# Attention and a feed-forward layer on one core: the order of the first 1040 operations from an explicit table

## The chip, the cores and the metric

The kernel runs on one core of a Trainium2 chip. A core has a matrix engine (TensorE, PE in the profile), a vector engine (VectorE, DVE), a scalar engine (ScalarE, ACT), a general engine (GpSimd, POOL) and an engine for synchronisation (SyncE, SP). Each works through its own list of instructions in the order in which the program gave them; they wait for each other through semaphores. Transfers are issued from the queues of POOL, SP and ACT and run on 16 DMA engines. PE multiplies from on-chip memory (SBUF) into its accumulators (PSUM), which DVE and ACT read.

The metric is the device time of one run in microseconds, as the median of several runs. A profile is one further execution with the hardware profiler on; its times are those of that execution.

## The reference

```python
def _attn_ref(q, k, v):                       # (8, 12, 448, 64) each
    S = q.shape[2]
    scale = 1.0 / np.sqrt(q.shape[-1])
    scores = scale * np.matmul(q, k.transpose(0, 1, 3, 2))
    attn = np.maximum(scores, 0.0) ** 2 / S
    return np.matmul(attn, v).astype(np.float32)

def _moe_ref(x, w_in, w_out):                 # (3584, 768), (768, 2048), (2048, 768)
    h = x @ w_in
    inv_sqrt2 = np.float32(1.0 / np.sqrt(2.0))
    g = 0.5 * h * (1.0 + erf(h * inv_sqrt2))
    return (g @ w_out).astype(np.float32)
```

`reference` runs the attention, moves the heads beside each other to a matrix of 3584 tokens by 768, and puts it through the two products with the exact GELU between them. Attention has a squared ReLU in place of a softmax.

## The kernel before

**Attention.** Eight batches are taken one after the other, each as three groups (`g`) of four heads. For a group, seven QK steps (`fn_qk`, line 674) each write four blocks of scores, 64 keys by 448 queries, into a PSUM buffer `ps`: four matmuls of 64x64 x 448 that run side by side, one in each quarter of the array. A ReLU with scaling follows, on ACT (`fn_relu`, line 686) or on DVE (line 688), into a buffer `a_sq`; DVE squares it in place (line 695). An AV step (line 735) sums 28 matmuls in the same 64x64 division into a PSUM buffer `pav`, and two copies (lines 451 on DVE and 453 on ACT) take it to `xT`. The buffers `ps` and `pav` come from one ring of three, named "w". Batch 0 is taken in half rows. The operands `qT` and `kT` of batches 0 and 1 are transposed on PE (lines 545 and 573); those of later batches by DMA transposes on the SP queue (line 600), after loads on the POOL queue (lines 407, 486 and 504). A small copy on POOL (`gate`, line 641) holds back the next loads until a group's transposes have landed.

**Feed-forward.** The first product of batches 0 to 4 is plain: six matmuls of 128x128 x 448 into a PSUM buffer `psh` (line 787), then GELU on ACT (line 797). The last three batches use a scheme with seven products in place of eight (Strassen's, after Winograd): products into `pb` (line 931), sums on DVE (line 965), GELU (line 974). The second product goes the same way in groups of 256 tokens (`add_group`): products p1, p6, p2, p7, p5, p4, p3 into `pso` (line 1101), sums v2, v3, c22, c21, c12 on DVE (line 1135) and copies. Its operands need sums of hidden rows (`s_sb`, line 1082) and of weights (`t_sb`, line 1038). The first 256 tokens are done plainly (line 1196). Results collect in a ring of three buffers `osb` and go out by stores on the SP queue (line 1062). `pso`, `psh` and the transposes share a ring of two PSUM buffers, "f".

**Division of the array.** Every operation of PE has a mode: "A" for QK and AV (64x64), "T" for transposes (128x64), "F" for the feed-forward (128x128). A list for PE (`pe_q`) weaves the feed-forward of earlier batches between the QK and AV steps of a later one.

**The order.** All work is first collected as 1427 `Op` objects (plus 8 fills, short matmuls on zeros that occupy PE early on) with their possible engines, durations, dependences and buffers. `Scheduler.run` then places them. `place` first takes the words of `ORDER`: P, A, D, G or S for PE, ACT, DVE, POOL or SP with the operation's number, or Z with the size of a fill. What the table doesn't name is placed by `pick` and `pick_pe`, which take the operation that can start first by the planner's own clock, with `SWITCH` added on PE at a change of mode. `run` does this `PASSES` times, each time with due times from the last placing (`deadlines`), keeps the best, sorts it by time, and only then calls each operation's function, which writes the instructions. So the planner's costs matter for the order alone. In the kernel before the table has 264 words, for the first part of the kernel.

Of the kernel before, what the change touches and what calls it, by code (L numbers as in the profile page):

```python
# [47 lines left out]
RELU_DVE = 0.8  # L48
DMA_FREE = 3.05
DMA_LAT = 2.13  # L50
SWITCH = 0.09
LEAD = 8
HALF_M = 6
PASS_BIAS = -0.4
SUM_BIAS = -0.3
# [1 line left out]
LEADS = {}  # L57
SHARES = (1.3, 1.0, 1.0, 1.0, 1.0, 1.0)
LAST = 256
PASSES = 5  # L60
PULL = 0.15
PULL_IN = 0.45
NEAR = 0.25
# [17 lines left out]


ORDER = """
A10 P11 D13 A16 D12 P17 D18 P14 G0 P42 A15 G1 P39 A40 G2 P19 D43 G3 D44 P21 A22 P33 D20 P36 G4
Z128 P54 G5 P25 A37 P23 A55 G6 P51 D34 P48 A24 A49 D26 D35 D56 D41 D38 A52 Z1056 P69 D70 G7
Z1024 P57 Z992 P63 A58 D53 Z448 P45 D50 P66 G8 G9 D59 A64 A46 P27 P31 D28 G117 D32 A67 D65 D68
A47 G118 P60 P78 G119 A61 P29 D30 G120 P81 A79 A82 D62 G121 G122 Z1088 P93 A94 D71 P108 Z544
P84 A85 Z992 P75 D109 A76 D83 D80 P72 P90 D73 P129 D95 P105 A74 G123 P102 A91 D130 A106 P131
D86 D77 G124 D132 P141 D92 A103 P111 P96 G125 A112 P165 P143 A97 D104 P156 D107 A166 A157 P87
D113 D98 P99 D110 D88 G126 A142 D89 P114 P174 P133 D100 G127 A101 A175 D115 D116 P159 A144  # L90
P168 D134 G128 P171 D169 A160 P135 D172 D173 D170 A136 G147 P251 P192 D193 P186 P162 A252 P145
D176 A163 A146 P243 P253 P180 P195 A187 A244 P198 P137 A254 G148 D164 D158 P139 G149 G150 A181
D167 G151 A199 D161 P183 D196 A184 P177 D138 D140 D188 G152 P189 P219 P245 P247 D194 A178 A190
S231 A220 D185 A179 P207 P216 A246 S229 D182 P213 D191 D197 P261 A248 A208 S232 P263 S228 D200
A214 P222 D217 P204 D221 D209 P201 D215 A262 A223 A264 P210 A211 P265 G153 S230 A266 P259 A260
P249 P255 D218 D205 A202 A250 A203 P257 D224 G154 A256 D206 D212 P225 P267 G155 A258
"""


# [14 lines left out]
class Scheduler:  # L114
# [99 lines left out]
    def run(self, fixed):  # L214


        best = None
        for _ in range(PASSES):
            self.reset()
            self.place(fixed)  # L220
            self.deadlines()
            end = self.free["PE"]
            if best is None or end < best[0]:
                best = (end, list(self.log))
        self.open, self.log = [], best[1]


        def at(x):
            est, op, eng = x
            if eng not in ("ACT", "DVE"):  # L230
                return est
            return est + next(lat for e, _, lat in op.engines if e == eng)

        for est, op, eng in sorted(self.log, key=at):
            op.fn(eng)

    def deadlines(self):
# [97 lines left out]
def kernel(  # L335
# [119 lines left out]
    def e_copy(n, psum=4):  # L455
# [4 lines left out]
    sch = Scheduler({"w": 3, "a": NA, "f": 2, "osb": 3, "s1": 1, "s2": 1, "s3": 1, "s4": 1,  # L460
                     "p": 1})
# [384 lines left out]
    def add_wsums(after, done):  # L846

        last = [o[0] for (bb, *_), o in list(Tq.items()) + list(Tk.items()) if bb == B - 1]
        last += [o for (bb, *_), o in QK.items() if bb == B - 2]
        add, sub = mybir.AluOpType.add, mybir.AluOpType.subtract  # L850

        def one(n, m0, op, a, b, deps):
            m1 = m0 + M1 // 2
            return sch.add(
                (("DVE", 0.95, 1.07),),
                lambda e: V.tensor_tensor(wcols(n, m0, m1), a(m0, m1), b(m0, m1), op=op),
                deps + last + after,
            )

        def part(i, j):  # L860
            return lambda m0, m1: wpart(i, j, m0, m1)

        def summed(n):
            return lambda m0, m1: wcols(n, m0, m1)

        for m0 in (0, M1 // 2):
            s1 = one(1, m0, add, part(0, 1), part(1, 1), [])
            s2 = one(2, m0, sub, summed(1), part(0, 0), [s1])
            s4 = one(4, m0, sub, part(1, 0), summed(2), [s2])
            s3 = one(3, m0, sub, part(0, 0), part(0, 1), [s1] + done)  # L870
            WS[m0] = {1: s1, 2: s2, 3: s3, 4: s4}
# [48 lines left out]
    def add_block(b, m4, y, ms, bank, x, t, TS, xs, old, half):  # L920

        tmp = {}

        def product(name, left, right, deps, first=False):
            def fn(e):
                if first and name not in bank:
                    bank[name] = w_pp.tile([128, 2, NB], F32, tag="w", name="pb")
                for z, m in enumerate(ms):
                    w, mm = left(m)
                    for k in range(K1):  # L930
                        nc.tensor.matmul(  # L931
                            bank[name][:, y, z * HS : z * HS + HS],
                            w[:, k, bass.ts(mm, 128)],
                            right()[:, k],
                            start=first and k == 0 and z == 0,
                            stop=k == K1 - 1,
                            skip_group_check=not first or z > 0,
                        )

            d = 2 * K1 * (HS / 2400 + 0.0025)  # L940
            return sch.add(
                (("PE", d, d + 0.24),), fn, deps, mode="F",
                need=("w",) if first and y == 0 else (),
            )

        def plain(i, j):
            return lambda m: (wpart(i, j), m)

        def summed(n):
            return lambda m: wtile(n, m)  # L950

        def ps(name):
            return bank[name][:, y, :S]

        def get(name):
            if name not in tmp:
                tmp[name] = apool.tile([128, S], F32, tag="a", name="part")
            return tmp[name]

        def passed(name, to, other, deps, need=()):  # L960
            def fn(e):
                if other is None:
# [40 lines left out]
        c12.frees = ("w",)  # L1003
        g12 = gelu(lambda: get("t"), 0, 1, [c12], ("a",))
        for name, o in (("a", c11), ("b", c21), ("c", c12)):
            bank.setdefault(("end", name), []).append(o)
        return [p1, p6, p2, p7, p5, p4, p3]
# [25 lines left out]
    def add_tsums():  # L1033

        def sub(n, c, a, b, deps):
            return sch.add(
                (("DVE", 0.95, 1.07),),
                lambda e: V.tensor_sub(tsum(n)[:, c], a()[:, c], b()[:, c]), deps, bias=TSUM_BIAS,
            )

# [24 lines left out]
    def add_group(g):  # L1065
# [13 lines left out]
        def sum_op(n, op, a, b, deps):  # L1079
            def fn(e):  # L1080
# [1 line left out]
                V.tensor_tensor(box["s", n], a(), b(), op=op)  # L1082

            o = sch.add(
                (("DVE", 0.69, 0.8),), fn, deps, need=(f"s{n}",), bias=SUM_BIAS
            )
            mine.append(o)
            return o
# [200 lines left out]
    o = early("ACT", lambda: nq[0][:, :4, : HC * D], q32, 5.3)  # L1289
# [70 lines left out]
    for b in range(2, B):  # L1360
# [9 lines left out]
        if b + 1 < B:  # L1370

            n = {2: 2}.get(b, 1)
# [91 lines left out]
```

## Time and profile before

| | us |
|---|---|
| median of 3 runs | 371.42 |
| lowest, highest | 371.38, 372.08 |
| the profiled execution | 371.65 |
| span of its profile | 369.5 |

Durations of single instructions that the prediction uses, by shape:

| line, engine | what | count | mean ns |
|---|---|---|---|
| L686 ACT | ReLU, 128x896 from PSUM | 138 | 924 |
| L688 DVE | ReLU, 128x896 from PSUM | 29 | 1089 |
| L695 DVE | square, 128x896 | 167 | 619 |
| L451 DVE | cast `pav` to `xT`, 128x448 | 38 | 617 |
| L453 ACT | the same | 4 | 535 |
| L453 ACT | copy `pso` to `osb` or `p_sb`, 128x384 | 17 | 478 |
| L1135 DVE | sum of `pso` and `p_sb` into `osb` | 39 | 556 |
| L1082 DVE | sum of hidden rows `s_sb` | 52 | 683 |

The page of a profile gives the busy time of each engine and its share of the span, then the chain of work that ended last, followed back from the last instruction. Lines of a timeline give start, length, engine, line, operation, and in brackets the idle time before it with what ended it. A DMA-issuing instruction on the SP queue is shown as SPq. Matmuls are pipelined, and their ends in the profile are modelled: a matmul's start is observed, its end is not.

### The profile page before, as it was taken

How to read it: one execution, taken by the hardware profiler on the slowest of the kernel's cores; microseconds unless marked ns; L12 is line 12 of the kernel's file. 1: busy time of each engine (PE TensorE's matmuls, PEld its weight loads, DVE VectorE, ACT ScalarE, POOL GpSimd, SP SyncE). 2: the span in 40 equal slices, each digit the busy share in tenths (PEclk: the TensorE clock that was granted, in tenths of full speed). 3: DMA queues.
4: the chain of work that ended last, by engine and by line, in shares of the span. 5: the costliest groups of instructions: out<-in, count | busy, mean ns of one | idle time of the engine just before them, and what ended most of it. 6: DMA issues, size and time to landing. Idle time of an engine off the chain costs nothing.

```text
span 369.5 us, 8514 instructions
## 1 busy us (share of the span) xinstructions
PE 361.4 (98%) x3573; PEld 222.9 (60%) x3573; DVE 280.9 (76%) x479; ACT 204.8 (55%) x313; POOL 63.5 (17%) x103
## 2 busy tenths in 40 slices
PE   8999999999999999999999999999999999999994
PEld 7675645455544455554455544447876897688663
DVE  3999930789887688997688979998778558765862
ACT  4998954755377745777764578853540353045200
POOL 8666304230112114040212000000000000000000
PEclk9999999999999999999999999999999999999998
DMA  9999999999999999999999992002002301210232
GB/s 174 195 202 204 202 185 167 194 202 171 159 217 208 163 163 204 189 167 162 180 169 117 164 200 64 2 1 87 2 0 87 88 0 46 87 40 2 85 87 85
DMA packets 89269, 47.27 MB, mean 128 GB/s; under 512 B 55312, under 2 KB 85776, under 8 KB 89232
## 3 DMA queue, kind: packets, MB, share of 16 engines
q0 software_dynamic: 32912, 22.47, 44.7%
q1 hardware_dynamic: 55952, 23.76, 36.6%
q8 instruction: 28, 0.46, 0.5%
q10 hardware_dynamic: 368, 0.51, 0.4%
q14 instruction: 9, 0.07, 0.1%
HBM read 45.61 MB, written 11.01 MB: 153 GB/s over the span
## 4 chain that ended last, share of the span: by engine, by line
PE 86%; DMA 3%; SPq 3%; DVE 2%; issue 1%; POOL 1%; ACT 1%; DVEq 0%; POOLq 0%; ACTq 0%
PE pso L1101 29%; PE psh L787 25%; PE pb L931 13%; PE ps L674 9%; PE pav L735 7%; SPq L600 3%; DMA nq<-in_q_dram 2%; PE pso L1196 1%; ACT a_sq L686 1%; DMA out_dram<-osb 1%; DVE osb L1135 1%; PE tp L573 1%; DVE part L965 1%; POOL v_sb L504 1%; PE tp L545 0%
## 5 line engine op out<-in xcount | busy, mean ns | idle before, releaser
L686 ACT ACTIVATE a_sq<-ps 128x896 bf16<-128x896 f32 x139 | 120.1, 921 | 32.0 <-PE ps L674 31.8
L695 DVE TENSOR_TENSOR a_sq<-a_sq 128x896 bf16<-128x896 bf16 (+1 forms) x169 | 98.2, 616 | 4.5 <-ACT a_sq L686 3.4
L787 PE MATMUL psh<-xT,win_sb 128*128 128x448 bf16 (+1 forms) x516 | 96.3, 340 | 0.0
L787 PEld LDWEIGHTS <-win_sb 128*128 128x128 bf16 x516 | 48.0, 98 | 45.1 <-issue 9.2
L797 ACT ACTIVATE h_sb<-psh 128x448 bf16<-128x448 f32 x80 | 43.8, 549 | 29.9 <-PE psh L787 29.9
L1101 PEld LDWEIGHTS <-s_sb 128*128 128x128 bf16 x424 | 40.4, 98 | 27.3 <-issue 3.2
L688 DVE TENSOR_SCALAR a_sq<-ps 128x896 bf16<-128x896 f32 (+1 forms) x30 | 32.1, 1073 | 24.8 <-PE ps L674 24.7
L965 DVE TENSOR_TENSOR part<-pb,part 128x448 f32<-128x448 f32 x60 | 34.6, 620 | 21.5 <-PE pb L931 21.5
L674 PE MATMUL ps<-qT,kT 64*64 64x448 bf16 (+1 forms) x756 | 48.6, 336 | 1.2 <-ACT a_sq L686 0.4
L1101 PEld LDWEIGHTS <-h_sb 128*128 128x128 bf16 x312 | 29.9, 98 | 21.8 <-issue 3.3
L1101 PE MATMUL pso<-wout_sb,s_sb 128*128 128x384 bf16 (+2 forms) x216 | 38.1, 320 | 0.1
L1101 PE MATMUL pso<-wout_sb,h_sb 128*128 128x384 bf16 x208 | 38.1, 326 | 0.0
L1101 PE MATMUL pso<-t_sb,s_sb 128*128 128x384 bf16 x208 | 38.1, 326 | 0.0
L735 PE MATMUL pav<-a_sq,v_sb 64*64 64x448 bf16 (+1 forms) x756 | 36.5, 329 | 0.0
L674 PEld LDWEIGHTS <-kT 64*64 64x64 bf16 x756 | 18.6, 105 | 24.7 <-issue 17.8
L974 ACT ACTIVATE h_sb<-part 128x448 bf16<-128x448 f32 x36 | 20.1, 578 | 20.2 <-DVE part L965 19.9
L451 DVE CAST xT<-pav 128x448 bf16<-128x448 f32 (+1 forms) x45 | 24.4, 581 | 7.9 <-PE pav L735 7.6
L1135 DVE TENSOR_TENSOR osb<-pso,p_sb 128x384 f32<-128x384 f32 x39 | 21.7, 556 | 9.8 <-PE pso L1101 5.3
L931 PEld LDWEIGHTS <-win_sb 128*128 128x128 bf16 x288 | 27.6, 98 | 2.3 <-issue 0.4
L735 PEld LDWEIGHTS <-v_sb 64*64 64x64 bf16 x756 | 21.0, 107 | 11.8 <-issue 1.6
L641 POOL COPY gate<-qT 128x16 bf16<-128x16 bf16 x15 | 4.3, 284 | 113.8 <-DMA qT<-nq 113.8
L931 PEld LDWEIGHTS <-ws 128*128 128x128 bf16 x216 | 20.7, 98 | 0.0
(61 smaller groups left out, 294.6 us busy)
## 6 DMA issues: line engine op xcount, KB each, us to landing
nk<-in_k_dram POOLq DMA_DIRECT2D x23, 224.0 KB, 6.7
nq<-in_q_dram POOLq DMA_DIRECT2D x21, 224.0 KB, 8.6
v_sb<-in_v_dram POOLq DMA_DIRECT2D x5, 672.0 KB, 15.0
out_dram<-osb SPq DMA_DIRECT2D x8, 336.0 KB, 3.0
v_sb<-in_v_dram POOLq DMA_DIRECT2D x9, 224.0 KB, 8.2
out_dram<-osb SPq DMA_DIRECT2D x7, 288.0 KB, 3.2
out_dram<-osb SPq DMA_DIRECT2D x8, 240.0 KB, 3.0
win_sb<-in_moe_w_in_dram POOLq DMA_DIRECT2D x8, 192.0 KB, 8.5
```

The source lines that it names most:

```text
L451: V.tensor_copy(dst, src)
L674: nc.tensor.matmul(ps[64 * j : 64 * j + 64, e, x * w : x * w + w], kT[r, g, i * 128 + 64 * j : i * 128 + 64 * j + 64], moving, start=True, ...
L686: A.activation(ar, ps, AF.Relu, scale=c_att)
L688: V.tensor_scalar(ar, ps, c_att, 0.0, op0=mybir.AluOpType.mult, op1=mybir.AluOpType.max,)
L695: V.tensor_mul(box["a2"][:, :, :used], ar, ar)
L735: nc.tensor.matmul(pav[0][o2 : o2 + 64, e, :w], vt[b][r, 2 * g + e, bass.ts(i, D)], box["a2"][r, y, o : o + w], start=(i == 0), stop=(i == ...
L787: nc.tensor.matmul(ph[:, x * n : x * n + n], win_sb[:, kd, bass.ts(m + x, 128)], xT[b][:, kd, c], start=(kd == 0), stop=(kd == KD - 1),)
L797: A.activation(h_ring()[:, m : m + nm, o + c.start : o + c.stop], box[0][:, :S].rearrange("p (x n) -> p x n", x=nm), AF.Gelu,)
L931: nc.tensor.matmul(bank[name][:, y, z * HS : z * HS + HS], w[:, k, bass.ts(mm, 128)], right()[:, k], start=first and k == 0 and z == 0, st ...
L965: V.tensor_add(get(to), ps(name), get(other))
L1101: nc.tensor.matmul(box[bank][:, n0:n1], left()[:, kf], right()[:, kf, n0:n1], start=bool(need) and kf == 0, stop=kf == K2 - 1, skip_group_ ...
L1135: V.tensor_add(out()[:, n0:n1], box[bank][:, n0:n1], other()[:, n0:n1])
```

## The change

The table `ORDER` becomes a new one of 1435 words: 1427 operations and the same 8 fills. Operations stand in it in a new sequence up to about the 1040th; from there on they stand as the planner had placed them before. Some operations change engine between ACT and DVE, as their letters say. The other edits are to the planner: `SWITCH` from 0.09 to 0.11, `PASSES` from 5 to 1, lower durations for three kinds of sums on DVE, no sort ahead of writing the instructions, and one more dependence, of the second half of a product bank on the first.

```diff
-SWITCH = 0.09
+SWITCH = 0.11
...
-PASSES = 5
+PASSES = 1
...
 ORDER = """
-A10 P11 D13 A16 D12 P17 D18 P14 G0 P42 A15 G1 P39 A40 G2 P19 D43 G3 D44 P21 A22 P33 D20 P36 G4
-Z128 P54 G5 P25 A37 P23 A55 G6 P51 D34 P48 A24 A49 D26 D35 D56 D41 D38 A52 Z1056 P69 D70 G7
...
-P249 P255 D218 D205 A202 A250 A203 P257 D224 G154 A256 D206 D212 P225 P267 G155 A258
+G0 G1 G2 G3 G4 G5 G6 A10 P11 D13 A16 P17 G7 D12 P14 D18 P42 P39 G8 P19 A15 P21 D43 P33 P36 D44
+A40 D20 Z128 A22 P54 G9 P25 P23 A37 D34 P51 D26 P48 A55 Z1056 D35 A24 P69 D56 Z1024 D41 A49
...
+S403 D428 P431 G409 D344 D338 S389 D341 P440 P437 D332 P345 S404 D430 A438 P443 D441 P446 S405
...
+G879 A830 G880 D827 S875 P733 G881 A907 D828 D831 P912 D825 P921 P832 D745 A913 P909 A732 D922
+P924 P735 D734 A833 A925 P737 A910 D743 A834 P936 D914 P918 P933 D736 P739 D738 S741 D744 A934
...
+P1419 D1418 S1424 P1420 D1421 S1425 D1422 S1426
 """
...
-        def at(x):
-            est, op, eng = x
-            if eng not in ("ACT", "DVE"):
-                return est
-            return est + next(lat for e, _, lat in op.engines if e == eng)
-
-        for est, op, eng in sorted(self.log, key=at):
+        for _, op, eng in self.log:
             op.fn(eng)
...
-                (("DVE", 0.95, 1.07),),
+                (("DVE", 0.86, 1.07),),
...
-            return sch.add(
-                (("PE", d, d + 0.24),), fn, deps, mode="F",
+            o = sch.add(
+                (("PE", d, d + 0.24),), fn, deps + bank.get(("first", name), []), mode="F",
                 need=("w",) if first and y == 0 else (),
             )
+            if first:
+                bank["first", name] = [o]
+            return o
```

More of the change, by code (lines that the diff above doesn't have):

```diff
@@ L83 @@
 ORDER = """
-A10 P11 D13 A16 D12 P17 D18 P14 G0 P42 A15 G1 P39 A40 G2 P19 D43 G3 D44 P21 A22 P33 D20 P36 G4
-Z128 P54 G5 P25 A37 P23 A55 G6 P51 D34 P48 A24 A49 D26 D35 D56 D41 D38 A52 Z1056 P69 D70 G7
[L86 to L95, printed above, removed]
@@ L96 @@
-P249 P255 D218 D205 A202 A250 A203 P257 D224 G154 A256 D206 D212 P225 P267 G155 A258
+G0 G1 G2 G3 G4 G5 G6 A10 P11 D13 A16 P17 G7 D12 P14 D18 P42 P39 G8 P19 A15 P21 D43 P33 P36 D44
+A40 D20 Z128 A22 P54 G9 P25 P23 A37 D34 P51 D26 P48 A55 Z1056 D35 A24 P69 D56 Z1024 D41 A49
+P57 Z992 D38 A52 P63 Z448 G117 D70 P45 A58 D53 P66 A64 D50 P27 A46 G118 P31 D59 P60 D28 A67
+G119 D32 A47 P78 P29 D65 G120 A61 P81 Z1088 D68 D30 A79 P93 D62 P108 Z544 D71 A82 P84 Z992
+G121 A94 P75 D109 P72 G122 D83 A85 P90 P129 D80 G123 D73 A76 P105 A74 P102 D95 G124 P131 D130
@@ new lines @@
+A91 P141 D86 A106 D77 P111 P96 D132 A103 P165 P143 D92 A112 D104 D107 A97 P156 D113 P87 G125
+D98 A166 P99 D110 G126 D88 A157 P114 A142 D100 A89 P174 G127 A101 P168 D115 P133 A144 P135
+A116 G128 D175 P171 P159 A169 D134 P251 D136 D170 A160 P145 D158 A172 D167 A252 P162 P186 D176
+P192 P243 A146 D161 G147 D173 A187 G148 P253 D193 A163 A244 D164 P195 G149 P180 P198 P137 A254
+G150 P139 D196 A181 P183 P177 G151 D138 A199 D140 A184 P189 P219 P245 D178 G152 A190 D185 P247
+G153 D194 A220 D179 A246 G154 P213 D188 P222 P204 P263 D221 A248 G155 D197 A214 D200 P265 D191
@@ new lines @@
+A205 D182 A264 P261 A223 A266 P216 D224 S231 P207 P201 D206 A262 A208 S229 P210 P259 D209 A217
+D215 S232 P255 D211 A260 P249 D212 D218 A256 D202 P225 A203 S228 A250 P257 S230 A226 P267 D227
+A258 P348 S234 A268 P350 S233 A349 P352 G237 A351 G238 P354 S235 A353 G239 P288 S236 P294 P282
+P358 A355 G240 G241 D289 P356 D283 A359 P360 D295 A357 D290 P306 P279 P276 D296 P362 A361 D307
+P364 D280 A363 P366 D277 A365 P368 A367 P370 A369 P300 P285 P291 G242 P372 A371 G269 D286 A292
+P374 G270 D284 A373 G271 P318 P303 D301 P312 G272 P376 D308 A375 G273 A304 D319 P378 D278 A377
@@ new lines @@
+P380 D313 A379 D293 G274 D314 D390 P382 D305 G275 D302 A381 D391 D287 D281 P330 P309 P297 S398
+D392 A331 D320 P315 S399 P384 D393 A298 D396 A310 S401 A383 D417 P387 D394 D419 A385 D311 A299
+D395 A316 D317 P324 P321 D418 A325 P333 D397 P327 A388 P421 D420 D322 S400 A328 D323 P423 D326
+A334 D422 S386 P339 P336 P342 P425 D424 D329 A343 D335 P427 S402 A426 D337 P429 G407 A340 G408
+S403 D428 P431 G409 D344 D338 S389 D341 P440 P437 D332 P345 S404 D430 A438 P443 D441 P446 S405
+P433 D432 A346 D347 A444 P509 A447 D434 P511 D439 G410 D448 S406 A510 G411 P449 D442 P452 G412
@@ new lines @@
+P455 P513 D562 A512 S435 D445 S436 A453 P515 D454 A450 A514 P517 D456 D451 P464 D457 P461 P458
+S541 A465 P467 D462 A518 P470 G413 S542 P519 A516 G414 A459 G415 P521 D471 S543 G416 D472 A520
+P523 D466 A468 D460 S544 A522 P479 D560 P476 P473 D469 P525 A524 D463 A477 P527 D480 A474 D478
+A526 P529 D475 D481 A528 P488 P485 P482 S545 A489 P494 D486 A530 P491 P531 D487 D483 P533 D495
+A532 S546 P535 D496 A484 D561 A492 P503 D490 P500 A534 P497 D493 P537 A536 G550 G551 S547 P564
+D498 G552 A538 D504 S548 P539 D499 A501 G553 A565 D505 P600 G554 D502 P603 P506 G555 S549 A601
@@ new lines @@
+P606 D604 A540 P609 P566 D563 A507 D602 P568 D607 D567 P570 D610 A569 A508 P572 D571 P624 P612
+P618 S704 P574 D580 D608 A613 D573 P576 S705 G556 A619 D581 G557 D582 P627 S706 D575 P615 G558
+P584 D614 G559 D577 S578 A616 D611 P586 S707 D605 A628 D617 A625 P636 D620 P630 S579 A585 P621
+D629 G713 A631 D637 P633 G714 P588 D587 S708 G715 A622 D626 D623 A634 P639 P642 P648 D583 P590
+D638 A640 D635 A589 D632 P592 D641 A643 D591 P651 A649 S709 D644 P657 P645 D593 A652 P666 D658
+P654 P594 D653 A646 D659 A655 D650 P596 A647 D667 S710 D595 P660 P766 P663 P672 D597 A661 D767
@@ new lines @@
+P674 A664 S711 D662 A673 D656 P676 D668 A675 D665 P772 P769 P669 S712 G716 D773 A770 P763 S598
+P775 A677 G717 P678 S599 D670 G718 A764 D771 P680 G719 D723 A776 S867 D768 A679 P790 P778 D765
+A671 P781 G720 P682 A681 D777 G721 D791 P684 G722 S868 D725 A683 P686 D779 A782 A685 P688 D783
+D780 D774 P787 P793 P784 D724 S869 A788 P799 D794 A687 P796 P690 A689 D795 D789 A797 P692 D798
+A691 P694 A693 P696 A785 A695 S870 P698 A786 A800 P802 P811 A697 P805 D801 P700 A699 A803 D812
+P702 S871 D792 A806 D804 P814 P817 D807 P808 A815 S872 P823 D818 A701 P820 P727 G876 D816 A703
@@ new lines @@
+G877 D809 S873 A821 G878 D726 P729 A810 D819 A728 D822 P826 D813 A824 P829 S874 P906 P731 D730
+G879 A830 G880 D827 S875 P733 G881 A907 D828 D831 P912 D825 P921 P832 D745 A913 P909 A732 D922
+P924 P735 D734 A833 A925 P737 A910 D743 A834 P936 D914 P918 P933 D736 P739 D738 S741 D744 A934
+P747 D908 G882 A937 D740 G883 P749 D938 A919 S978 G884 D935 A748 G885 D926 P942 P930 S742 P915
+P751 D750 A931 D943 S979 P753 D920 A916 A752 D746 P755 D923 S980 D911 D944 P948 P945 D917 P927
+D888 A949 D754 P939 P757 D950 A928 D886 D756 P759 A946 D887 A940 D758 A929 P835 D932 D947 D941
@@ new lines @@
+S981 P957 P954 P951 A836 D958 A955 P960 P963 D760 P837 D959 A961 D952 P839 D956 A953 S982 A838
+P966 D964 P972 P969 D962 P841 A840 S983 D889 A973 D965 P843 S984 A842 D967 P847 A970 S985 A844
+P845 D971 D968 S761 D974 P990 P987 D1067 P975 S986 A991 P993 D988 A846 P996 S762 P849 D992
+A848 D1068 A976 D1070 P851 A997 D989 A850 P853 A994 A977 D995 P1005 P1002 A852 P999 P855 A854
+D1006 A1003 P859 D1004 A1000 D998 A856 P857 D1007 D1001 P1011 P1014 P1008 D1059 A858 A1012
+P1017 D1015 P1026 P861 A1009 D1063 A860 P863 D1060 A1018 D1010 P1020 A1027 P1029 D1061 P1023
@@ new lines @@
+A862 P865 D1016 A864 D1019 P890 A1021 D1028 D1022 A866 P892 D1062 A1024 A891 D1013 P894 D1025
+A1030 D1069 D893 P1035 D1031 P1038 P1032 D1064 A895 A1036 D1066 P1041 D1037 A1039 P1044 P896
+D1033 A1042 D1034 D1040 P898 A1045 D1043 D897 P1047 D1046 P1050 P1053 P900 D899 A1048 D1139
+P902 D1049 A1051 D1140 A1054 P1071 D1052 D1055 P1056 D901 S904 A1072 D903 S905 P1088 D1141
+P1073 D1057 P1090 A1089 D1058 P1143 D1074 D1091 P1075 D1065 P1092 A1144 P1077 D1142 A1076
+D1179 P1094 A1093 D1180 P1079 D1078 P1096 D1095 P1145 D1080 D1097 A1081 P1082 D1181 A1098
@@ new lines @@
+P1099 D1146 P1085 D1083 P1102 D1100 A1084 P1105 D1086 A1101 P1122 D1103 A1087 P1107 D1182
+A1106 P1124 A1123 P1147 A1104 D1108 D1125 P1109 P1126 A1148 P1111 A1110 P1128 A1127 P1113
+D1112 P1130 D1129 P1149 D1114 D1131 A1115 P1116 A1132 P1133 D1150 P1119 D1117 P1136 D1134
+A1118 P1151 D1120 A1135 D1137 A1121 P1153 D1291 A1138 D1292 D1152 P1155 D1159 D1154 S1157
+P1163 D1160 D1156 S1158 P1165 D1161 D1164 P1167 D1162 D1166 D1293 P1169 D1294 A1168 P1171
+D1170 P1173 D1253 D1172 P1175 D1251 D1174 S1177 P1183 D1252 P1200 D1176 S1178 P1185 A1184
@@ new lines @@
+D1254 P1202 A1201 P1255 D1186 D1203 P1187 P1204 A1256 P1189 A1188 P1206 A1205 P1191 D1190
+P1208 D1207 P1257 D1192 D1209 A1193 P1194 A1210 P1211 D1258 P1197 D1195 P1214 D1212 A1196
+P1217 D1198 A1213 P1234 D1215 A1199 P1219 A1218 P1236 A1235 P1259 A1216 D1220 D1237 P1221
+P1238 A1260 P1223 A1222 P1240 A1239 P1225 D1224 P1242 D1241 P1261 D1226 D1243 A1227 P1228
+A1244 P1245 D1262 P1231 D1229 P1248 D1246 A1230 P1263 D1232 A1247 D1249 A1233 P1265 A1250
+D1264 P1267 D1271 D1266 S1269 P1275 D1272 D1268 S1270 P1277 D1273 D1276 P1279 D1274 D1278
@@ new lines @@
+P1281 D1280 P1283 D1282 P1285 D1365 D1284 P1287 D1363 D1286 S1289 P1295 D1364 P1312 D1288
+S1290 P1297 A1296 D1366 P1314 A1313 P1367 D1298 D1315 P1299 P1316 A1368 P1301 A1300 P1318
+A1317 P1303 D1302 P1320 D1319 P1369 D1304 D1321 A1305 P1306 A1322 P1323 D1370 P1309 D1307
+P1326 D1324 A1308 P1329 D1310 A1325 P1346 D1327 A1311 P1331 A1330 P1348 A1347 P1371 A1328
+D1332 D1349 P1333 P1350 A1372 P1335 A1334 P1352 A1351 P1337 D1336 P1354 D1353 P1373 D1338
+D1355 A1339 P1340 A1356 P1357 D1374 P1343 D1341 P1360 D1358 A1342 P1375 D1344 A1359 D1361
@@ L97 @@
+A1345 P1377 A1362 D1376 P1379 D1383 D1378 S1381 P1387 D1384 D1380 S1382 P1389 D1385 D1388
+P1391 D1386 D1390 P1393 D1392 P1395 D1394 P1397 D1405 D1396 P1399 D1403 D1398 S1401 P1407
+D1404 D1400 S1402 P1409 D1406 D1408 P1411 D1410 P1413 D1412 S1423 P1415 D1414 P1417 D1416
+P1419 D1418 S1424 P1420 D1421 S1425 D1422 S1426
 """
@@ L1036, in sub @@
             return sch.add(
-                (("DVE", 0.95, 1.07),),
+                (("DVE", 0.86, 1.07),),
                 lambda e: V.tensor_sub(tsum(n)[:, c], a()[:, c], b()[:, c]), deps, bias=TSUM_BIAS,
@@ L1084, in sum_op @@
             o = sch.add(
-                (("DVE", 0.69, 0.8),), fn, deps, need=(f"s{n}",), bias=SUM_BIAS
+                (("DVE", 0.6, 0.8),), fn, deps, need=(f"s{n}",), bias=SUM_BIAS
             )
```

## The prediction

> **What bounds the kernel now.** I read the page's busy times first, then the busy times by stage, then the chain of work that ended last, and at its two odd places the timeline.
>
> ```profile
> span 369.5 us, 8514 instructions
> ...
> PE 361.4 (98%) x3573; PEld 222.9 (60%) x3573; DVE 280.9 (76%) x479; ACT 204.8 (55%) x313; POOL 63.5 (17%) x103
> ...
> PE 86%; DMA 3%; SPq 3%; DVE 2%; issue 1%; POOL 1%; ACT 1%; DVEq 0%; POOLq 0%; ACTq 0%
> ```
>
> TensorE is the bound. No other engine can set the end on average, so an order gains only by making PE's own work shorter or by taking out a wait of PE. The stages differ (columns: stretch, length, then busy time of PE, weight load, DVE, ACT and POOL, clock, DMA share, GB/s):
>
> ```profile
> 0.00:32.00 32.00, 29.60 (x609) 22.08 (x613) 25.35 (x51) 25.77 (x38) 22.36 (x36) 1.00 1.23 192
> 32.00:99.00 67.00, 67.00 (x612) 36.29 (x609) 46.20 (x71) 41.83 (x65) 18.79 (x30) 1.00 1.26 188
> 99.00:250.00 151.00, 150.03 (x1420) 76.32 (x1419) 128.32 (x215) 101.95 (x143) 22.41 (x37) 1.00 1.05 146
> 250.00:369.50 119.50, 114.76 (x939) 88.22 (x936) 81.00 (x145) 35.28 (x68) 0.00 (x0) 0.99 0.18 54
> ```
>
> PE is full in all but the first stage and the tail; DMA is full up to 250 us. The chain's pieces (start, length, what) show what a change of array division costs; psh is in 128x128, ps in 64x64:
>
> ```profile
> 54.33 10.32 PE psh L787 x54
> ...
> 107.05 0.69 PE ps L674 x12
> 107.74 3.51 PE psh L787 x18
> 111.25 0.50 PE ps L674 x8
> ```
>
> From 18 to 54 psh matmuls takes 6.81 us more, 0.189 each; 18 of them should take 3.41 but take 3.51, so 0.10 belongs to the run and not to its matmuls. Four more ps matmuls take 0.19; eight should take 0.38 but take 0.50, so 0.12. A run in 128x128 and a run in 64x64 together carry 0.22 to 0.23 for two changes: **0.113 us a change**.
>
> Now the wait that matters most for where a saving counts (chain pieces again):
>
> ```profile
> 84.91 6.86 SPq L600
> ...
> 91.87 2.97 SPq L600
> ...
> 94.93 0.53 SPq L1062
> ...
> 95.52 3.17 DMA out_dram<-osb
> ...
> 98.78 0.56 DVE osb L1135
> ```
>
> and the timeline of PE after it:
>
> ```profile
> 97.64 1.46 PE L1101 MATMUL pso<-t_sb,s_sb 128*128 128x384 bf16 x8
> ...
> 99.39 1.46 PE L1101 MATMUL pso<-t_sb,h_sb 128*128 128x384 bf16 x8 [0.29 <-DVE osb L1135]
> ```
>
> This is p4 of output group 1. It waits for v3, v3 for an osb buffer, the buffer for the store of a plain tile, and that store (L1062) stands behind transposes (L600) in SP's queue. Starts are 1.75 us apart where eight such matmuls need 1.30: PE stands 0.45 us. One later place is in the region that changes:
>
> ```profile
> 190.57 0.57 PE L674 MATMUL ps<-qT,kT 64*64 64x448 bf16 x8
> ...
> 191.00 3.43 ACT L686 ACTIVATE a_sq<-ps 128x896 bf16<-128x896 f32 x4 [1.15 <-PE ps L674]
> ...
> 192.29 0.87 PE L674 MATMUL ps<-qT,kT 64*64 64x448 bf16 x8
> ```
>
> Two QK steps take 0.57 at 190.57 and 0.87 at 192.29: the last waits 0.30 us for a score buffer whose ReLU is second in line on ACT. PE's columns hide it, since a matmul's shown end covers the gap.
>
> **What the Trainium skill says.** "TensorEngine Tiling (Array Packing)", section Key Properties: changing the tiling mode, not just the tile, drains TensorE. The trace agrees, with 0.113 us each. "TensorE: Matmul & The Clock Gate", section Architectural detail: ACT and DVE take instructions strictly in order. The trace agrees: DVE's row at 98.78 stood 0.96 us, and the two squares queued behind it begin only at 99.25. "Perfetto Trace Analysis", section Tensor Engine Instruction: the matmul end is an estimate, so I use starts; the hidden 0.30 above is such a case.
>
> **The change part by part.**
>
> *Constants, PASSES, the sort, the new dependence.* The table now names all 1427 operations and the 8 fills, so nothing is left for the planner to choose; SWITCH and the durations decide nothing. The new dependence ties two products on PE that are in that order anyway. Zero; the last 396 operations of the built program are identical.
>
> *POOL and SP* keep their orders: 84 of 84 operations each, DMAs included. No step passes a load, a transpose or a store. Before 99 us the waits of these queues that end last are on DMA landings, not on PE (the SP queue waits 20.5 us for nk before the transposes quoted). So v3's buffer comes at the same time, and **p4 stays at 99.39**. What PE saves before that it waits away at p4.
>
> *Changes of division.* Counted along PE's instructions in the two built programs: 118 before, 109 after. Up to p4 48 become 45; the set of operations done by then is the same, so these 3 (0.34 us) are lost. From p4 on 70 become 64, the last by the place that is at 238 us before: 6 x 0.113 = **0.68 us**, on the path, since PE runs without a longer break to the end. Bounds: 0 if each run's first matmul then waits for its buffer, 0.68 otherwise; I take it whole.
>
> *The wait at 192.5.* Before, the QK pair after the AV step waits for two ReLUs in a row on ACT (0.92 each). After, the two ReLUs in question stand on ACT and DVE, side by side; DVE first does an s_sb sum (0.68) and then the ReLU (1.09), which ends about when the second QK is due. Between 0 and 0.30; I take **0.2**.
>
> *Engines.* ReLUs on DVE go from 30 to 50, on ACT from 139 to 119; plain copies move the other way, 26. From p4 on: 16 ReLUs to DVE (16 x 1.09 = 17.4 us), 20 xT casts and 5 PSUM copies to ACT (20 x 0.617 + 5 x 0.556 = 15.1). DVE gains 2.3 us in a stage where it has 151.0 - 128.3 = 22.7 free; ACT loses about 1.8. Hidden by PE on the sum; locally between -0.1 (the ring of three score buffers is freed sooner) and +2.7 us (each of the 16 frees its buffer 1.09 - 0.92 = 0.17 later and PE waits for it each time). I take 0.
>
> *Waits that stay:* the QK step at 244.54 (0.43 shown, for ReLUs on ACT) and the product after 275 us keep the order around them, and cost the same.
>
> Sum: 0.68 + 0.2 = 0.9 us; the span goes from 369.5 to 368.6. The profiled execution took 371.65 outside its span, the three runs have a median of 371.42, so the forecast is 371.42 - 0.9 = **370.5 us**.
>
> **The rivals.**
> - *All nine changes count.* If SP's queue reaches the store sooner, p4 moves with PE: 9 x 0.113 + 0.30 = 1.3, so 370.1. Against it: SP's four transposes ahead of that store begin at the landing of nk at 82 us, with nothing of PE before them.
> - *The saving turns into waits.* Grouping QK steps asks for score buffers in quicker succession, and there are three. A wait of 0.3, as at 192.5, at three new places takes the 0.9 back: 371.4. For it: such waits stand at 103, 192.5 and 244 already. Against: a group stays at two or three QK steps, as in the pieces of 0.69 above.
> - *Slower: the ReLUs moved to DVE.* DVE is 85% busy from 99 to 250 us and works strictly in order, with squares of 0.62 in the queue. If a ReLU there ends 0.17 late and PE waits, five of the 16 eat the 0.9; from ten on it is slower. Twelve give 2.0 - 0.9 = 1.1: 372.5. Against: in before 15 such ReLUs stand in this stage and PE shows only the waits named.
> - *The table isn't followed:* excluded, the built program has its order.
>
> **How the numbers follow.** Forecast 0.62, all nine 0.10, waits 0.16, slower 0.12. The forecast's own range is 369.9 to 371.0 (nothing at 192.5 and a third of the changes lost, or both whole and small waits gone). To hold 8 in 10 it reaches to the waits on one side and to all nine on the other: 369.7 to 371.7. A measurement here tells 0.2%, 0.74 us, from no change: faster means under 370.7. Five sixths of the forecast (0.52) and all nine (0.10) make 0.62; the rest of the forecast and the waits 0.26; slower 0.12.
>
> **What would show it.** p4 of group 1 again at 99.4 with a longer wait ahead of it (about 0.8); PE's work from there to the first pb product 0.9 shorter; the QK pair after 192 us at 0.57 to 0.67; 109 changes with the same pieces of 0.69 and 3.51. It is wrong if p4 moves, if QK rows wait at new places for ReLUs of L688, or if stores slip and transposes land after their QK steps.

## The result, and the profile after

| | before | after |
|---|---|---|
| median | 371.49 us (6 runs) | 370.1 us (6 runs) |
| lowest, highest | 371.12, 372.13 | 369.5, 371.11 |
| profiled execution, span | 371.65, 369.5 | 370.26, 368.5 |

The ratio is 0.996, with a 95% interval of 0.9942 to 0.9977: 1.4 us faster, where 0.9 was forecast.

The head, the busy times and the shares of the chain on the page of the kernel after:

```profile
span 368.5 us, 8472 instructions
...
PE 360.2 (98%) x3573; PEld 223.6 (61%) x3573; DVE 285.1 (77%) x473; ACT 199.2 (54%) x319; POOL 63.1 (17%) x103
...
PE 77%; DMA 8%; SPq 5%; DVE 4%; POOL 2%; issue 1%; ACT 1%; DVEq 0%; POOLq 0%; ACTq 0%
```

PE remains the bound, at the same 98%. DVE has 4.2 us more work and ACT 5.6 us less, as the ReLUs moved. The chain has gone from 86% PE to 77%: it runs through the transposes, the store and v3 at p4 as before, but in this execution it goes back from there through a load of `wout_sb`, 16.32 us from 61.43 on, where before it went back through PE. The busy times by stage, with the same columns as for the kernel before:

```profile
0.00:32.00 32.00, 29.55 (x605) 22.50 (x606) 24.68 (x50) 25.79 (x40) 22.37 (x36) 1.00 1.24 192
32.00:99.00 67.00, 66.74 (x612) 36.19 (x612) 48.77 (x72) 38.65 (x61) 18.68 (x30) 1.00 1.26 188
99.00:249.10 150.10, 149.25 (x1421) 76.77 (x1420) 130.86 (x209) 99.63 (x152) 22.06 (x38) 1.00 1.01 147
249.10:368.50 119.40, 114.63 (x938) 88.14 (x936) 80.76 (x145) 35.13 (x68) 0.00 (x0) 1.00 0.18 54
```

Busy PE falls by 1.2 us, but it cannot tell work from waiting, because a matmul's modelled end covers gaps. Starts can. The place of p4 first, in the timeline of the kernel after (lines have moved: L1166 is L1101 of before, L1200 is L1135, L736 is L674, L748 and L750 are L686 and L688):

```profile
97.68 1.46 PE L1166 MATMUL pso<-t_sb,s_sb 128*128 128x384 bf16 x8
99.08 0.56 DVE L1200 TENSOR_TENSOR osb<-pso,p_sb 128x384 f32<-128x384 f32 x1 [1.97 <-DMA out_dram<-osb]
...
99.69 1.46 PE L1166 MATMUL pso<-t_sb,h_sb 128*128 128x384 bf16 x8 [0.54 <-DVE osb L1200]
```

and the pieces of its chain up to 104 us (start, length, what):

```profile
85.07 7.09 SPq L662
...
92.25 2.76 SPq L662
...
95.10 0.53 SPq L1127
...
95.69 3.31 DMA out_dram<-osb
...
99.08 0.56 DVE osb L1200
...
100.08 1.69 DVE a_sq L757 x3
101.77 0.47 DVE osb L1200
102.24 1.01 DVE a_sq L750
...
103.29 0.38 PE ps L736 x4
```

Transposes, store, v3, p4: the same chain as before. p4 starts 2.01 us after the product ahead of it, 1.30 is that product's own length, so PE waits 0.71 us (0.45 before). The chain goes on past p4: the squares behind v3 push a sum and a ReLU back, and the QK step at 103.29 waits for that ReLU. This second wait of PE, 0.30 us, stands in both kernels.

From p4 on the two differ by a fixed amount. The last product whose start I use (of L1101, or L1166) begins 264.84 us after p4 before and 263.50 us after: **1.34 us less**. The QK pair after 190 us in the kernel after:

```profile
190.82 0.57 PE L736 MATMUL ps<-qT,kT 64*64 64x448 bf16 x8
...
191.26 0.92 ACT L748 ACTIVATE a_sq<-ps 128x896 bf16<-128x896 f32 x1 [1.48 <-PE ps L736]
191.54 1.08 DVE L750 TENSOR_SCALAR a_sq<-ps 128x896 bf16<-128x896 f32 x1
...
192.55 0.55 PE L736 MATMUL ps<-qT,kT 64*64 64x448 bf16 x8
...
193.03 1.47 PE L1166 MATMUL pso<-t_sb,s_sb 128*128 128x384 bf16 x8
```

The pair took 0.87 at 192.29 us before, and takes 0.55 now: the two ReLUs run side by side. In the kernel before, the product behind the pair stands here:

```profile
193.09 1.48 PE L1101 MATMUL pso<-t_sb,s_sb 128*128 128x384 bf16 x8
```

From the start of the pair to the start of that product it was 0.80 us before and is 0.48 now, **0.32 us less**. The pieces of the chain after 107 us have the old prices, 0.69, 3.51 and 0.50; there are fewer of them:

```profile
107.35 0.69 PE ps L736 x12
108.04 3.51 PE psh L849 x18
111.55 0.50 PE ps L736 x8
```

### The profile page after: what moved, and what is told of

The parts are those of the page before. It is cut to its first block, busy times and chain, and to the rows that moved or that the text cites. A ratio compares the mean times of both kernels' runs of the same rounds, so it can differ in the third digit from the quotient of the medians.

```text
span 368.5 us, 8472 instructions
## 1 busy us (share of the span) xinstructions
PE 360.2 (98%) x3573; PEld 223.6 (61%) x3573; DVE 285.1 (77%) x473; ACT 199.2 (54%) x319; POOL 63.1 (17%) x103
## 4 chain that ended last, share of the span: by engine, by line
PE 77%; DMA 8%; SPq 5%; DVE 4%; POOL 2%; issue 1%; ACT 1%; DVEq 0%; POOLq 0%; ACTq 0%
PE pso L1166 30%; PE psh L849 19%; PE pb L993 13%; PE ps L736 8%; PE pav L797 6%; SPq L662 5%; DMA wout_sb<-in_moe_w_out_dram 4%; DMA nq<-in_q_dram 2%; DVE a_sq L757 1%; DVE t_sb L1103 1%; DMA out_dram<-osb 1%; DMA qT<-nq 1%; ACT a_sq L748 1%; DVE part L1030 1%; PE tp L635 1%
## 5 line engine op out<-in xcount | busy, mean ns | idle before, releaser
L748 ACT ACTIVATE a_sq<-ps 128x896 bf16<-128x896 f32 (+1 forms) x119 | 104.5, 921 | 37.0 <-PE ps L736 36.7
L757 DVE TENSOR_TENSOR a_sq<-a_sq 128x896 bf16<-128x896 bf16 (+1 forms) x169 | 96.8, 614 | 9.4 <-ACT a_sq L748 8.8
L750 DVE TENSOR_SCALAR a_sq<-ps 128x896 bf16<-128x896 f32 (+1 forms) x50 | 53.4, 1076 | 17.2 <-PE ps L736 17.1
L1166 PEld LDWEIGHTS <-s_sb 128*128 128x128 bf16 x424 | 40.7, 98 | 26.6 <-issue 2.0
L736 PE MATMUL ps<-qT,kT 64*64 64x448 bf16 (+1 forms) x756 | 47.8, 336 | 0.7 <-ACT kT L515 0.3
L1166 PEld LDWEIGHTS <-h_sb 128*128 128x128 bf16 x312 | 29.6, 98 | 22.6 <-issue 4.6
L1166 PE MATMUL pso<-wout_sb,s_sb 128*128 128x384 bf16 (+2 forms) x216 | 38.1, 320 | 0.1
L1166 PE MATMUL pso<-wout_sb,h_sb 128*128 128x384 bf16 x208 | 38.1, 326 | 0.0
L1166 PE MATMUL pso<-t_sb,s_sb 128*128 128x384 bf16 x208 | 38.1, 326 | 0.0
L736 PEld LDWEIGHTS <-kT 64*64 64x64 bf16 x756 | 18.6, 105 | 23.0 <-issue 16.7
L1200 DVE TENSOR_TENSOR osb<-pso,p_sb 128x384 f32<-128x384 f32 x39 | 21.6, 554 | 11.2 <-PE pso L1166 6.7
L1166 PE MATMUL pso<-t_sb,h_sb 128*128 128x384 bf16 x104 | 19.1, 326 | 0.5 <-DVE osb L1200 0.5
```

What stands on the lines that cost most here:

```text
L736: nc.tensor.matmul(ps[64 * j : 64 * j + 64, e, x * w : x * w + w], kT[r, g, i * 128 + 64 * j : i * 128 + 64 * j + 64], moving, start=True, ...
L748: A.activation(ar, ps, AF.Relu, scale=c_att)
L750: V.tensor_scalar(ar, ps, c_att, 0.0, op0=mybir.AluOpType.mult, op1=mybir.AluOpType.max,)
L757: V.tensor_mul(box["a2"][:, :, :used], ar, ar)
L1166: nc.tensor.matmul(box[bank][:, n0:n1], left()[:, kf], right()[:, kf, n0:n1], start=bool(need) and kf == 0, stop=kf == K2 - 1, skip_group_ ...
L1200: V.tensor_add(out()[:, n0:n1], box[bank][:, n0:n1], other()[:, n0:n1])
```

## The experiments

The numbers of all runs stand together here; the readings follow one by one. "Wait at p4" is the distance from the product ahead of it to p4, less 1.30. "From p4" is the distance from p4 to the QK step at 107 us, and "to the end" from there to the start of the last product; both come from starts in the timelines. The last columns are medians, and beside each that of the kernel before in the same comparison.

| kernel | order to 107 us, after it | p4 at | wait at p4 | from p4 | to the end | median, runs | before |
|---|---|---|---|---|---|---|---|
| before | old, old | 99.39 | 0.45 | 7.59 | 257.25 | 371.49, 6 | |
| before_again | old, old | 99.27 | 0.26 | 7.59 | 257.26 | 371.63, 12 | 371.85 |
| after | new, new | 99.69 | 0.71 | 7.59 | 255.91 | 370.1, 6 | 371.49 |
| after_again | new, new | 98.69 | 0.13 | 7.59 | 255.91 | 369.76, 5 | 371.66 |
| early_old | old, new | 99.24 | 0.28 | 7.59 | 255.91 | 369.91, 20 | 371.55 |
| early_old_again | old, new | 99.65 | 0.43 | 7.59 | 255.91 | 370.14, 18 | 371.85 |
| late_old | new, old | 99.89 | 1.06 | 7.59 | 256.97 | 370.86, 14 | 371.55 |
| late_old_again | new, old | 99.69 | 0.70 | 7.59 | 258.26 | 371.21, 22 | 371.85 |
| early_old_p4 | old to p4, new | 99.70 | 0 | 7.27 | 255.91 | 370.12, 22 | 371.66 |
| store_act | new, new | 99.55 | 0 | 7.27 | 259.06 | 369.87, 22 | 371.55 |
| store_act_before | old, old | 99.50 | 0 | 7.49 | 256.97 | 371.69, 22 | 371.55 |
| split12 | new, new | 99.41 | 0.31 | 7.59 | 258.67 | 372.72, 9 | 371.66 |
| relu_act | new, new | 99.51 | 0 | 7.28 | 256.27 | 370.29, 5 | 371.66 |
| swap338 | new, new | 99.88 | 0.12 | 7.59 | 256.18 | 369.63, 12 | 371.85 |

### Which half holds the gain: early_old and late_old

Each half of the change alone. The table of the first kernel has the old sequence and the old engines up to the QK step at 107 us (operation 449) and the new ones after it, the second kernel the other way round. For early_old, as it stands to the kernel after:

```diff
-G0 G1 G2 G3 G4 G5 G6 A10 P11 D13 A16 P17 G7 D12 P14 D18 P42 P39 G8 P19 A15 P21 D43 P33 P36 D44
+G0 G1 G2 G3 G4 G5 G6 A10 P11 G7 D13 A16 P17 G8 D12 P14 D18 P42 P39 P19 A15 P21 D43 P33 P36 D44 A40
...
+P429 D338 A343 D428 P431 D341 D344 G413 G414 D430 P437 G415 P440 D560 P345 G416 D432 S435 A438
```

> The old order (and old engines) of everything up to the QK step at 107 us, a little past p4; the new order from there. Theory (p4 is pinned by the store behind the transposes, so what PE saves before it is waited away): as fast as the new kernel, 370.1, with p4 at 99.4 to 99.7 and its wait at about 0.45 in place of 0.71. Rival (all nine changes count): three changes come back, 0.34 slower than new, 370.4.

> The new order up to the same QK step, the old one from there. Theory: no gain, 371.5, p4 again at about 99.5 and the waits near 192.5 (0.30) and 244 (0.6) back. Rival (all nine count): three changes are kept, 371.1.

early_old: ratio 0.9948 (0.9929 to 0.9967). late_old: ratio 0.9977 (0.9957 to 0.9998). The end follows the order after 107 us: 255.91 with the new one and 256.97 with the old one, whatever stood ahead. The new half alone carries the larger part of the gain. But late_old, which was to be the kernel before from 107 us on, is 0.28 shorter there than the kernel before, and its median 0.69 under it. Both points were run again:

> The kernel before, unchanged, with a profile of its own. Theory (the 0.62 us wait at 244.5 us in the first profile holds 0.2 to 0.3 of chance, a copy of ACT that began 0.3 late once): the wait is 0.40, and from the QK step that follows p4 (operation 449, at 107 us) to the last product it takes 257.0. Rival (the late copy belongs to that order): 257.25 again.

> The new order and engines up to the QK step at 107 us, the old ones from there. Theory (ahead of p4 three changes of division fewer are worth at most 0.34, and less where p4 waits for the store): operation 449 to the last product 257.0 again, as in the kernel before, and a time 0 to 0.34 under the kernel before beside it. Rival (the early part gives what its first comparison showed): 0.7 under.

> The old order and engines up to the QK step at 107 us, the new ones from there. Theory: operation 449 to the last product 255.9 again, 1.05 less than the kernel before, and a time 1.0 to 1.1 under the kernel before beside it. Rival (the first comparison's 1.6 is right, and something unseen in the profiles comes on top): 1.6 under.

before_again: ratio 0.9997 (0.9971 to 1.0022). It shows 257.26, as the first profile did, so my theory of one late copy by chance falls. In the profile of before_again:

```profile
242.27 0.48 ACT L453 COPY osb<-pso 128x384 f32<-128x384 f32 x1 [2.06 <-issue]
242.65 3.35 ACT L686 ACTIVATE a_sq<-ps 128x896 bf16<-128x896 f32 x4
...
244.43 0.38 PE L674 MATMUL ps<-qT,kT 64*64 64x448 bf16 x4 [0.43 <-ACT a_sq L686]
```

and in that of late_old, where L734 is L674 and L513 is L453:

```profile
242.61 0.48 ACT L513 COPY osb<-pso 128x384 f32<-128x384 f32 x1 [1.77 <-issue]
242.99 3.35 ACT L746 ACTIVATE a_sq<-ps 128x896 bf16<-128x896 f32 x4
...
244.77 0.38 PE L734 MATMUL ps<-qT,kT 64*64 64x448 bf16 x4 [0.23 <-ACT a_sq L746]
```

The same copy in the same order: ACT stands idle 2.06 us ahead of it in the one and 1.77 in the other, with no releaser in either. So ACT begins this copy, and the ReLUs behind it, 0.28 us later in both profiles of the kernel before, and in none of the three profiles of kernels that share its order after 107 us and differ elsewhere (late_old, late_old_again, store_act_before). It belongs to the kernel before, and the change removes it. What makes ACT late there stays open. The traces hold one more difference at this place. From 241 to 246 us the DMA engines move a single packet in both profiles of the kernel before, 0.7 us behind the start of the copy, and none in the other three. It is a fetch of instructions (queue, kind, packets, MB, share of the engines):

```profile
q14 instruction: 1, 0.01, 0.5%
```

Whether it has to do with the late copy is not shown: in late_old a like fetch stands at 249.44, and ACT is not late there.

early_old_again: 255.91 for the third time; ratio 0.9948 (0.9933 to 0.9963). late_old_again: 258.26, of which 1.30 is a wait for a late store at 155 us (below); without it 256.96, as expected. Its ratio is 0.9977 (0.9962 to 0.9992), 0.64 us by the medians.

### Is the price of a change real: split12

Twelve QK steps behind p4 go one feed-forward step later, which adds 24 changes of division (64 to 88 from p4 on) and nothing else. Three of the twelve:

```diff
-P455 P513
+P513 P455
...
-P491 P531
+P531 P491
...
-P609 P566
+P566 P609
```

> The order after, with 12 QK steps behind p4 moved one feed-forward step later, so that the array changes its division 24 times more; same work, same engines. Theory (a change costs 0.113 us and PE has no slack from p4 on): 24 x 0.113 = 2.7 us, p4 to the end 263.5 + 2.7 = 266.2, time 372.8. Rival (fewer changes are not what made the kernel faster, the waits that went with the old order are): p4 to the end 263.5 to 264.0, time 370.1 to 370.6.

Ratio 1.0032 (1.0015 to 1.005): slower than the kernel before. From p4 to the last product it takes 266.26, that is 2.76 us more for 24 changes, **0.115 each**. The chain of split12 shows the first place:

```profile
107.07 0.50 PE ps L734 x8
107.58 1.24 PE psh L847 x6
108.82 0.31 PE ps L734 x4
109.13 2.38 PE psh L847 x12
```

These four pieces hold the 12 ps and 18 psh matmuls of the 0.69 and 3.51 above, and take 4.43 in place of 4.20: 0.23 for two changes. Followed from place to place the starts slip by 0.23 at each of the twelve, and nothing of it is taken back by a later wait. The rival, that changes cost nothing by themselves, falls.

### What removed the wait at 192.5: relu_act

One ReLU goes back to ACT, behind the one it had stood behind before:

```diff
-D745 A913 P909 A732 D922
+D745 A913 A922 P909 A732
```

> The order after, with one ReLU (the second of the pair at 191 us) back from DVE to ACT, behind the first. Theory (two ReLUs in a row on ACT made the wait at 192.5): the QK step after them starts 0.3 later than now, 0.85 after the one before it where it is 0.55, and p4 to the end becomes 263.8; time 370.4. Rival (the new order of steps took the wait away, not the engine): the pair stays at 0.55 and p4 to the end at 263.5.

Ratio 0.9962 (0.9947 to 0.9977). The timeline of relu_act:

```profile
190.34 0.57 PE L734 MATMUL ps<-qT,kT 64*64 64x448 bf16 x8
...
190.77 1.73 ACT L746 ACTIVATE a_sq<-ps 128x896 bf16<-128x896 f32 x2 [1.48 <-PE ps L734]
...
192.06 0.87 PE L734 MATMUL ps<-qT,kT 64*64 64x448 bf16 x8
```

Both ReLUs in a row on ACT (x2), and the pair takes 0.87 again. "To the end" is 256.27, 0.36 more than with the ReLU on DVE: 0.30 in the pair and, by the starts, 0.08 ahead of the product after it, less 0.01 inside that product. So it was the engine. In the kernel before that product came only about 0.02 late, so what the change gained here is the 0.32 above. p4 to the end reads 263.55 and not 263.8, because in this execution p4 did not wait and the wait at 103 us was absent: 7.28 in place of 7.59.

### What pins p4: store_act, store_act_before and after_again

The store that v3 waits for leaves SP's queue and goes out from ACT's, right after the copy that fills its buffer, in the kernel after and in the kernel before:

```diff
-sch.add((("SP", 0.6, 2.8),), lambda e: store_rows(t, osbs[t, "plain"]), [ev],
+sch.add((("SP", 0.6, 2.8),), lambda e: store_rows(t, osbs[t, "plain"],
+        queues=[nc.scalar] * 2 if t == 0 else None), [ev],
```

> The new kernel, with one store taken from behind the transposes: the first plain tile goes out from ACT's queue as soon as its copy is done, in place of SP's. Theory: the store lands near 91 us, p4 starts 1.31 after the product before it, its wait of 0.71 goes and stays gone to the end: 369.4; up to 0.3 more if the wait at 103 us goes with it. Rival (p4 waits for something else, such as DVE's queue): p4 stays at 99.5 or later and the time at 370.1.

> The same move of one store in the kernel before. Theory: p4's wait of 0.45 goes, 371.0. Since nothing pins p4 now, the two orders should differ by more than before: 1.4 plus 0.25 or so. Rival: nothing moves, 371.5.

In both, p4 follows the product ahead of it by 1.30: the wait is gone. But this cannot be put down to the move of the store. ACT issues the two DMAs from 88.0 us on, 7 us before SP did, and they do not land near 91. The larger one, issued by SP in the kernel after, by ACT in store_act and by ACT in store_act_before (KB, us from issue to landing):

```profile
out_dram<-osb SPq DMA_DIRECT2D x1, 336.0 KB, 3.6
...
out_dram<-osb ACTq DMA_DIRECT2D x1, 336.0 KB, 9.6
...
out_dram<-osb ACTq DMA_DIRECT2D x1, 336.0 KB, 10.3
```

The second of the two lands at 97.87 in store_act (99.00 in the kernel after) and at 98.62 in store_act_before (98.70 in the kernel before); issued by SP it lands between 97.90 and 99.20 in the other profiles. ACT's queue moves no packet of it before 92 us. In store_act v3 then waits for its product and no longer for the store; in store_act_before it still waits for the store, and starts as late as in the kernel before (98.78). First store_act, then store_act_before:

```profile
98.45 0.56 DVE L1198 TENSOR_TENSOR osb<-pso,p_sb 128x384 f32<-128x384 f32 x1 [0.66 <-PE pso L1164]
...
98.74 0.56 DVE L1198 TENSOR_TENSOR osb<-pso,p_sb 128x384 f32<-128x384 f32 x1 [0.36 <-DMA out_dram<-osb]
```

PE also comes later, to the product ahead of p4 at 98.25 and 98.20, 0.57 us later than in the kernels after and before. It comes so late in relu_act (98.21) and early_old_p4 (98.40) too, where the store was not moved, and p4 does not wait there either. So these two runs do not show that the store's place in SP's queue holds p4. The times, which were to be 369.4 and 371.0, do not show it either (369.87 and 371.69): store_act ratio 0.9961 (0.9949 to 0.9974), store_act_before 1.0006 (0.9991 to 1.0022). What the traces do show is that the landing holds p4. In each of the ten profiles in which p4 waits, v3 starts 0.08 us after the store's landing and p4 0.61 after v3. Why the store lands when it does, from either queue, stays open.

> The kernel after, unchanged, beside the other kernels of this set. Theory: the first p4 of group 1 is pinned by the store behind SP's transposes, at 99.4 to 99.9 us, and everything from it to the end takes 263.5 us again, with a wait of 0.35 near 243.5; time 370.1 to 370.3. Rival: what was seen after p4 was one profile's luck; then p4 to the end would differ from 263.5 by more than 0.3.

Ratio 0.9955 (0.9937 to 0.9972). "To the end" is 255.91 to the hundredth, but p4 comes at 98.69 with a wait of only 0.13. The expected 99.4 to 99.9 was missed: the pin is no fixed time. From a QK step at 20 us to p4 the profiles with the new early order take 78.29 to 79.54 us and those with the old one 78.60 to 79.31. SP's four transposes ahead of the store begin at 82.40 in the profile of after and at 81.59 in that of after_again.

### The wait at 103 us: early_old_p4 and swap338

early_old_p4 keeps the old order up to p4 itself and no further; in it one of the squares stands ahead of v3 on DVE:

```diff
-S403 D428 P431 G409 D344 D338 S389 D341 P440 P437 D332 P345 S404 D430 A438 P443 D441 P446 S405
+P429 D338 A343 D428 P431 D344 D341 P440 P437 P345 D430 A438 P443 D441 P446 P433 D432 A346 D347
```

> The order and engines of the kernel before up to the first p4 of group 1 itself, those of the kernel after from there on. Theory (what comes ahead of p4 is waited away there, and the old order brings SP's store some 0.3 us sooner): p4 at 99.2 to 99.5, p4 to the end 263.2 to 263.5, with the wait of 0.30 at 103 us gone; time 369.6 to 369.9. Rival (the new order ahead of p4 is worth its three changes of division, 0.34 us): 370.4 or more.

Ratio 0.9974 (0.9956 to 0.9992). The wait at 103 us is gone in the profile, and so is the one at p4 (v3 there waits for its product, not for the store), and the chain is nearly all PE:

```profile
PE 93%; DVE 2%; DMA 2%; POOL 1%; issue 1%; ACT 0%; DVEq 0%; POOLq 0%; ACTq 0%
```

The median does not show a gain over the kernel after (370.12, where 369.6 to 369.9 was expected), so it is no better version. And p4's wait and the one at 103 us went together, as in relu_act, where four squares stand behind v3 in place of two. In relu_act:

```profile
98.21 1.46 PE L1164 MATMUL pso<-t_sb,s_sb 128*128 128x384 bf16 x8
98.59 0.56 DVE L1198 TENSOR_TENSOR osb<-pso,p_sb 128x384 f32<-128x384 f32 x1 [0.95 <-DMA out_dram<-osb]
...
99.51 0.65 PE L1164 MATMUL pso<-t_sb,h_sb 128*128 128x384 bf16 x3
```

From v3 to the QK step at 103 us it is 4.21 us in all ten profiles in which p4 waits, with the old order and with the new one, and 4.23 in relu_act. So this QK step follows v3 through the work queued behind it on DVE. When p4 starts 0.61 after v3, the QK step comes 3.60 after p4, where PE alone needs 3.31 (early_old_p4, store_act and relu_act): 0.30 of wait. The two waits are one delay of v3, seen twice.

> The order after, with one square of DVE (operation 338) ahead of the sum v3 (operation 344) that waits for the store, in place of behind it. Theory (the squares queued behind the waiting v3 make the wait of 0.30 at 103 us): that wait is gone, p4 to the end is 263.2 in place of 263.5, p4 itself is not moved by it; time 369.5. Rival (the wait at 103 us comes from the score buffers, not from v3's place in DVE's queue): 263.5 and the wait of 0.30 stay.

This edit missed its aim. Operation 344 is a square like 338; v3 is operation 428, so two squares behind v3 changed places and nothing passed it. The run counts as one more of the kernel after: ratio 0.994 (0.9918 to 0.9962), 7.59 from p4, 255.94 to the end without a wait of 0.24 at 154.8 us. Whether moving a square ahead of v3 would take the 0.30 away was not tried.

## Why the prediction was right, and where it was not

**Right: the price of a change, and that six of them count.** 24 added changes give 0.115, against 0.113 foretold. Six saved ones make 6 x 0.115 = 0.69, all on the path. "TensorEngine Tiling (Array Packing)", section Key Properties, of the Trainium skill says that a changed tiling mode drains TensorE and gives no figure; here it is 0.115 us a change, between 64x64 and 128x128.

**Right in kind, too small: the wait at 192.5.** The split between ACT and DVE removed it, but I took 0.2 because the DVE ReLU seemed to end about when the QK step is due. It ends in time: the term is 0.32 by the starts in the two kernels, and relu_act, which takes the split back, loses 0.36.

**Wrong: "waits that stay".** The QK step at 244.54 was put down as unchanged, since its surroundings keep their order. It cost 0.62 before by starts (the 0.43 of the prediction ends at a modelled end) and costs 0.35 after. The copy that ACT begins late in the kernel before makes 0.28, as before_again and late_old show: 0.23 of it here and 0.05 at the QK step just ahead. The order of the work around it gave no hint of it. About 0.05 is left for the new order (0.40 to 0.35). With these the sum from p4 on is 0.69 + 0.32 + 0.28 + 0.05 = 1.34, as measured. No other step of PE between p4 and the last product is off its usual length by more than 0.02 us in one of the two kernels and not in the other.

**Only partly right: "p4 stays", and three changes are lost.** In the first profile p4 came no earlier and waited 0.71, where about 0.8 was foretold. The reason given, that the store stands behind the transposes in SP's queue, is not shown: issued from ACT 7 us sooner, it landed 0.1 and 1.1 us sooner. Over the profiles, leaving the two kernels with a moved store aside, PE is ready for p4 78.41 us after the QK step at 20 us with the new early order (mean of seven, wait taken off) and 78.71 with the old one (mean of five): 0.31 sooner, near 3 x 0.113. The waits are 0.43 and 0.28 in the mean, so about half of it is waited away. The scatter of single executions is as large as the effect. The medians agree no better: with the old late half the new early one is 0.69 and 0.64 under the kernel before, 0.28 of it the copy; with the new late half, swap338 is 0.51 under early_old_again beside it. So the early part gives something between nothing and 0.5 us, and this stays open. The rival "all nine count" is then neither shown nor excluded. That it gave 370.1, the median measured, speaks for it by luck only: the 1.34 from p4 on holds none of the three changes.

**Right: the moved ReLUs cost nothing.** The groups of the kernel after (line, engine, tiles, count, then busy time, mean ns):

```profile
L748 ACT ACTIVATE a_sq<-ps 128x896 bf16<-128x896 f32 (+1 forms) x119 | 104.5, 921 | 37.0 <-PE ps L736 36.7
...
L750 DVE TENSOR_SCALAR a_sq<-ps 128x896 bf16<-128x896 f32 (+1 forms) x50 | 53.4, 1076 | 17.2 <-PE ps L736 17.1
```

Twenty more ReLUs on DVE, and no new place where PE waits over 0.12 us: from p4 on, the places with such waits are 103, 192, 244 and 276 us before, and 103, 243 and 275 after. The rival with ReLUs of 0.17 too late each, and the one with three new waits of 0.3, fall with this.

The forecast of 0.9 was short by 0.12 at 192.5 and 0.33 at 244. The first measurement, 1.4, agrees with the 1.34 that two profiles of each kernel show from p4 on. The later ones lie higher: 1.9 for after_again, whose interval takes in 1.34, and 2.2 for swap338, whose interval begins at 1.41. The rest is not explained.

## What to carry to other kernels

When PE is the bound, count the changes of array division in the two orders, price one from the pieces of the chain, and ask for each saved one whether a wait with a time of its own stands behind it. Read waits of PE from starts, not from modelled ends, and do not take a wait as unchanged because its surroundings keep their order: an engine may be late there for a reason that the order does not tell. Two ReLUs that release buffers for one pair of QK steps are better on two engines where PE waits for the second: here that was worth 0.32 us.

## What was unexpected

- ACT begins one copy 0.28 us later in the kernel before than in two others with the same order around it, in each of their profiles.
- A store issued 7 us sooner, from another engine's queue, landed hardly sooner: it took 9.6 and 10.3 us in place of 3.6.
- A DMA store can land so late that PE stands. In the execution of store_act that was profiled, which at 372.94 us was the longest of its runs, v3 of a later group waited 3.36 us for one:

```profile
154.40 0.56 DVE L1198 TENSOR_TENSOR osb<-pso,p_sb 128x384 f32<-128x384 f32 x1 [3.36 <-DMA out_dram<-osb]
155.54 0.57 PE L795 MATMUL pav<-a_sq,v_sb 64*64 64x448 bf16 x7 [1.88 <-DVE a_sq L755]
...
157.01 0.38 PE L734 MATMUL ps<-qT,kT 64*64 64x448 bf16 x4 [0.71 <-DVE a_sq L748]
```

  The squares behind v3 on DVE came late, and PE lost 3.1 us in all. late_old_again lost 1.30 at the same place, swap338 0.24, the other profiles nothing. What delays the store was not tested.
- From 107 us on, executions of different kernels with the same order agree to 0.01 us where no store is late (255.91 in five of them), the late copy of the kernel before apart; the rest of the scatter between their profiles lies ahead of it, where this QK step comes between 106.28 and 107.48 us.
